# Queries turned on the host, keys and values as token rows, smaller score banks, a spread-out ranking and earlier first operands of the cosine layer

## The chip, the cores and the metric

The kernel runs on one core of one Trainium2 chip. The metric is the time of one execution on the device in microseconds (us), lower is better. The core has five engines that run their own instruction lists in order and wait for each other by semaphores: PE (matrix multiplies, from weights that are loaded into the array first; the loads are shown as PEld), DVE (vector), ACT (scalar), POOL and SP, which here mostly issues DMAs.

## The reference

```python
scores = (1 / sqrt(64)) * q @ k.T          # 8 batches, 8 heads, 576 tokens, head size 64
ret    = scores * gamma[h] ** (i - j)      # only for i >= j, else 0 (a decaying causal mask)
x      = (ret @ v)                         # -> 4608 tokens x 512
logits = x @ w_gate                        # 8 experts; each token goes to its best one
out[t] = gate[t] * (relu(x[t] @ w1[e]) @ w2[e])
h      = out @ w_in;  result = (h * cos(h)) @ w_out     # 512 -> 2048 -> 512, all tokens
```

All inputs are fp32 except the two matrices of the cosine layer, which arrive as 64-bit floats and are converted in the kernel.

## The kernel before

The program has three stages that follow one another.

**Attention and routing.** Each batch of 576 tokens is cut in five chunks, four of 128 tokens and one of 64, so there are 40 steps. Because the mask decays by a fixed factor, a chunk needs only itself (`intra`) and a carried 64x64 state per head (`inter`, from `sbd`). In iteration `i` the code issues `transposes(i+1)` (queries and decayed keys turned on PE into the PSUM tile `tp`, copied out by ACT), `scores(i)` (PE into `sc`, masked by DVE into `pT`), `decay_k(i+2)` (DVE), sometimes `unit_split` (an expert weight cut in two fp32r parts by ACT and DVE, 8 of the 40 iterations), `inter(i-1)` and `intra(i-1)` (PE into `xps`, scaled by DVE into `xt`), and `rows(i-2)` (PE turns the result back to token rows and makes the logits, into `rw`; ACT copies the rows out, then DVE sums the logits into `lgt`). `sc` and `rw` are the same PSUM buffer of two banks, with one copy, so the scores of an iteration wait until DVE has read the logits of the iteration before. Once a batch `route`, `place` and `spread`, in three iterations that follow each other, give every token a slot in its expert's list; they are small instructions on DVE and POOL. Loads of `q`, `k`, `v` are issued by SP four iterations ahead.

**Experts.** The experts are ranked by their count, and each takes a window of tokens in two halves (`hf`): `layer1` eight times, `layer2` four times, so 24 pieces, counted by `i`. At the first expert four bursts on DVE (`offsets`, `slots`, `excess`, and `turn_slots`, which has a PE transpose) finish the ranking behind the first four pieces; their scratch tile `room` takes one of the two `cvw` buffers. A background list (`bg`, some steps after each piece) converts the cosine layer's weights on DVE and ACT, with its loads (`conv_load`, into `cvw`) on SP. At the last expert SP loads the cosine layer's weights: `wide_unit` (8 pieces of 1 MB) and `ws_load(0)`, `ws_load(1)` (1.75 MB each, tile `wquad`, two buffers).

**Cosine layer.** A branch (`tc.If(late > 0)`, L1043, not taken here) stands ahead of it. Then 72 iterations (nine tiles of 512 tokens, eight column groups) run: seven products of 256 columns from `wquad` and operands that `enter` has put into a ring (`near`, `far`), with a cosine gate on ACT and DVE and the second matrix product `acc` (L1180). Four of the seven operands of a tile are differences (`turned`). The operands of the first tile are made behind the branch, the differences on POOL; those of later tiles at points of the loop named in `ahead`. `ws_load(i + 2)` is issued in iteration `i`.

Of the kernel before, what the change touches and what calls it, by code (L numbers as in the profile page):

```python
# [103 lines left out]

@with_exitstack
def attn_moe_kernel(ctx, tc, q, k, v, wg, w1, w2, win, wout, ctab, out):
    nc = tc.nc
    B = q.shape[0]
# [93 lines left out]
    with ExitStack() as actx:  # L202
# [3 lines left out]
        ps2 = actx.enter_context(tc.tile_pool(name="ps2", bufs=2, space=PSUM))  # L206
# [46 lines left out]
        for i in range(2):  # L253
            t = ap1.tile([P, NCH, E], F32, name=f"lgt{i}")
            nc.gpsimd.memset(t, 0.0)
            lgt.append(t)
# [5 lines left out]
        def load(i, nm):  # L262
            b, c = steps[i]
            o, n = CH[c]
            src = {"q": q, "k": k, "v": v}[nm]
            t = ap3.tile([P, H, D], F32, tag="ld" + nm, name="ld" + nm, bufs=6 if nm == "v" else 4)
            nc.sync.dma_start(out=t[:n], in_=src[b, :, o:o + n, :].rearrange("h t d -> t h d"))
            st[i][nm] = t

        def loads(i):  # L270
            for nm in "qkv":
                load(i, nm)
# [10 lines left out]
        def transposes(i):  # L283
            b, c = steps[i]
            o, n = CH[c]
            s = st[i]
            for nm in ("q", "kp"):
                pt = ps2.tile([P, 4, P], F32, tag="tp", name="tp")
                for j in range(4):
                    nc.tensor.transpose(pt[:, j, :n], s[nm][:n, 2 * j:2 * j + 2, :].rearrange("p a d -> p (a d)"),  # L290
                                        ident[:n, :n])
                t = ap3.tile([P, 4, P], F32, tag=nm + "T", name=nm + "T")
                nc.scalar.copy(out=t[:, :, :n], in_=pt[:, :, :n])
                s[nm + "T"] = t

        def scores(i):
# [4 lines left out]
            two = ps1.tile([P, 8, P], F32, tag="sc", name="sc")  # L301
            scs = [two[:, 0:4], two[:, 4:8]]
# [53 lines left out]
        def rows(i):  # L356
            b, c = steps[i]
            o, n = CH[c]
            two = ps1.tile([P, 8, P], F32, tag="sc", name="rw").rearrange("p (j a) t -> p j (a t)", a=2)
            for j in range(4):  # L360
                mm(out=two[:, j, 0:RW], lhsT=xts[i % 3][:, j, :], rhs=wgi[:, j, :], start=(j % 2 == 0), stop=True,
                   skip_group_check=True)
            x = ap3.tile([P, 4, P], F32, tag="xs", name="xs")
            if i < NS - 1:
                nc.scalar.copy(out=x[:n], in_=two[:n, :, 0:P])
            nc.vector.tensor_reduce(out=lgt[b % 2][:n, c, :], in_=two[:n, :, P:RW].rearrange("p j e -> p e j"),
                                    axis=AX.X, op=ALU.add)
            if i == NS - 1:
                nc.scalar.copy(out=x[:n], in_=two[:n, :, 0:P])
# [5 lines left out]
        def route(i0, n):  # L375

            b, c0 = steps[i0]
            L = lgt[b % 2][:, c0:c0 + n, :]
            sh = [P, n, E]
            mx = ap2.tile([P, n], F32, tag="mx", name="mx")  # L380
# [129 lines left out]
        load(0, "q")  # L510
        nc.sync.dma_start(out=ct, in_=ctab[:, :C_MASK])
        load(0, "k")
        nc.sync.dma_start(out=ca[:, :C_TRI - C_MASK], in_=ctab[:, C_MASK:C_TRI])
        load(1, "q")
        load(1, "k")
        load(0, "v")
        load(1, "v")
# [78 lines left out]
    def y_first():  # L596
        for g in range(2):
            nc.sync.dma_start(out=first[g], in_=ydT[2 * g * P:(2 * g + 2) * P, 0:512].rearrange("(a p) t -> p a t", p=P))

    with ExitStack() as mctx:  # L600
# [83 lines left out]
        cv = mctx.enter_context(tc.tile_pool(name="cv", bufs=1))  # L684
# [151 lines left out]
        def pick_slots(out, x):  # L836
            V.tensor_tensor(out=big, in0=hot.unsqueeze(2).to_broadcast([P, E, NBLK, E]),
                            in1=x.rearrange("p (e c) -> p c e", c=NBLK).unsqueeze(1).to_broadcast([P, E, NBLK, E]),
                            op=ALU.mult)
            V.tensor_reduce(out=out.rearrange("p (r c) -> p r c", c=NBLK), in_=big, axis=AX.X, op=ALU.add)  # L840

# [440 lines left out]
```

## Time and profile before

| | us |
|---|---|
| median of 3 runs (1454.59 to 1456.05) | 1454.84 |
| the profiled execution, its own time | 1457.35 |
| its span, first to last instruction | 1455.6 |
| PE busy | 1408.5 (97%) |
| PEld busy | 1306.1 (90%) |
| DVE busy | 959.1 (66%) |
| ACT busy | 714.3 (49%) |
| POOL busy | 229.2 (16%) |

The busy share is a mean over three stages with different limits, and a PE that the profile calls busy need not be at its peak. The profile's 40 slices show the granted PE clock at full speed except around 0 to 30, 200 to 270 and 673 to 691 us, that is at the start and at the two changes of stage. The span and the time of the profiled execution differ by 1.75 us, and that execution is 2.5 us above the median.

### The profile page before, as it was taken

The page shows a single profiled execution, that of the slowest core. Times are in us where ns is not written, and L with a number is a line of the kernel's source. Part 1 is how long each engine was busy: PE and PEld are TensorE (multiplying, and loading weights), DVE is VectorE, ACT ScalarE, POOL GpSimd, SP SyncE. Part 2 cuts the span into 40 slices and gives each one's busy share as a digit, 9 for nine tenths or more (in the row PEclk, how much of TensorE's full clock was granted, in tenths as well). Part 3 has the DMA queues.
Part 4 walks back from the last instruction along what each step waited for, and adds up shares of the span by engine and source line. Part 5 has one row for each costly group of instructions (what it writes and reads, how often), then busy time and mean ns, then how long its engine had stood idle before and what let it go on. Part 6 is the DMA issues. An engine that isn't in the chain of part 4 may idle for free.

```text
span 1455.6 us, 29059 instructions
## 1 busy us (share of the span) xinstructions
PE 1408.5 (97%) x11587; PEld 1306.1 (90%) x11587; DVE 959.1 (66%) x1900; ACT 714.3 (49%) x1405; POOL 229.2 (16%) x338
## 2 busy tenths in 40 slices
PE   8999987999999999997999999999999999999998
PEld 6888876999999999997899999999999999989896
DVE  4676765766777676843766667676766767666654
ACT  2344431445544545532655656555555556555544
POOL 3243341032221313201001010000101000010101
PEclk9999996999999999997999999999999999999999
DMA  9899853585777668776546464655656465555541
GB/s 190 205 220 225 216 128 97 166 263 176 250 221 225 218 188 265 255 256 254 203 163 249 158 254 153 226 187 185 227 178 235 167 231 173 205 202 193 191 165 67
DMA packets 179740, 292.25 MB, mean 201 GB/s; under 512 B 120612, under 2 KB 129264, under 8 KB 169360
## 3 DMA queue, kind: packets, MB, share of 16 engines
q1 hardware_dynamic: 166672, 248.33, 53.5%
q0 software_dynamic: 12928, 42.02, 8.4%
q8 instruction: 92, 1.51, 0.4%
q14 instruction: 48, 0.39, 0.1%
HBM read 238.85 MB, written 51.47 MB: 199 GB/s over the span
## 4 chain that ended last, share of the span: by engine, by line
PE 46%; issue 5%; DMA 1%; POOL 0%; DVE 0%; ACT 0%; POOLq 0%; ACTq 0%
PE acc L1180 24%; PE hps L1105 22%; DMA wquad<-ws 1%; POOL out_dram L1162 0%; DVE near L1090 0%; DVE far L1090 0%; POOLq L1278 0%; ACT ka L1135 0%; ACT near L1089 0%; POOL spare L143 0%; ACT orow L1160 0%; ACT gh L1146 0%; ACTq L1089 0%; POOLq L1162 0%
## 5 line engine op out<-in xcount | busy, mean ns | idle before, releaser
L1180 PE MATMUL acc<-wunit,gh 128*128 128x512 f32 x1152 | 358.4, 392 | 1.4 <-ACT gh L1146 1.4
L1180 PEld LDWEIGHTS acc<-wunit,gh 128*128 128x128 f32 x1152 | 207.3, 189 | 37.7 <-ACT gh L1146 1.8
L1105 PEld LDWEIGHTS hps<-far,wquad 128*128 128x128 f32 x1824 | 232.6, 192 | 6.2
L1105 PE MATMUL hps<-far,wquad 128*128 128x256 f32 x1824 | 237.3, 283 | 0.0
L1180 PE MATMUL acc<-wunit,gl 128*128 128x512 f32 x576 | 224.7, 390 | 0.0
L662 PE MATMUL hps<-xT,wunit 128*128 128x256 f32 (+6 forms) x1536 | 211.7, 299 | 0.7 <-ACT xT L647 0.7
L662 PEld LDWEIGHTS hps<-xT,wunit 128*128 128x128 f32 x1536 | 209.4, 191 | 1.3 <-ACT xT L647 1.1
L677 PE MATMUL hps<-hh,wunit 128*128 128x256 f32 (+6 forms) x1024 | 209.1, 299 | 0.2 <-ACT hh L665 0.2
L1105 PE MATMUL hps<-near,wquad 128*128 128x256 f32 x1200 | 161.8, 287 | 5.4 <-DVE near L1090 2.8
L1105 PEld LDWEIGHTS hps<-near,wquad 128*128 128x128 f32 x1200 | 156.7, 195 | 11.5 <-DVE near L1090 3.7
L677 PEld LDWEIGHTS hps<-hh,wunit 128*128 128x128 f32 x1024 | 165.3, 189 | 0.6 <-ACT hh L665 0.4
L677 PE MATMUL hps<-hl,wunit 128*128 128x256 f32 (+6 forms) x512 | 152.1, 297 | 0.8 <-DVE hl L666 0.7
L1162 POOL DMA_INDIRECT out_dram<-orow,perm x36 | 35.2, 977 | 727.9 <-DVE orow L1158 716.4
L1180 PEld LDWEIGHTS acc<-wunit,gl 128*128 128x128 f32 x576 | 108.2, 188 | 25.3 <-DVE gl L1148 1.6
L1142 DVE SCALAR_TENSOR_TENSOR sa<-sa,quad 128x512 f32<-128x512 f32 x144 | 99.1, 688 | 42.8 <-ACT sa L1140 42.8
L1146 ACT CAST gh<-sa 128x512 fp32r<-128x512 f32 x144 | 89.6, 622 | 72.5 <-DVE sa L1142 72.5
L1148 DVE TENSOR_TENSOR gl<-sa,gh 128x512 fp32r<-128x512 f32 x144 | 99.0, 688 | 23.0 <-ACT gh L1146 17.5
L1116 DVE TENSOR_TENSOR part<-hps,part 128x256 f32<-128x256 f32 x72 | 30.6, 425 | 120.1 <-PE hps L1105 120.0
L1137 DVE SCALAR_TENSOR_TENSOR sa<-quad,ka 128x512 f32<-128x512 f32 x144 | 99.0, 687 | 12.2 <-ACT ka L1135 12.2
L795 DVE TENSOR_TENSOR wunit<-wst,wunit 128x512 fp32r<-128x512 f32 x112 | 75.8, 687 | 36.2 <-ACT wunit L794 36.1
L677 PEld LDWEIGHTS hps<-hl,wunit 128*128 128x128 f32 x512 | 97.0, 189 | 1.4 <-DVE hl L666 1.4
L1139 ACT ACTIVATE sa<-sa 128x512 f32<-128x512 f32 x144 | 91.3, 634 | 9.0 <-DVE sa L1137 8.8
(196 smaller groups left out, 1900.0 us busy)
## 6 DMA issues: line engine op xcount, KB each, us to landing
wquad<-ws SPq DMA_DIRECT2D x72, 1792.0 KB
wst<-in_moe_w_dram SPq DMA_DIRECT2D x64, 512.0 KB
ws<-cvo POOLq DMA_DIRECT2D x56, 256.0 KB, 4.5
ldq<-in_q_dram SPq DMA_DIRECT2D x32, 256.0 KB
ldk<-in_k_dram SPq DMA_DIRECT2D x32, 256.0 KB
ldv<-in_v_dram SPq DMA_DIRECT2D x32, 256.0 KB
xd<-xs SPq DMA_DIRECT2D x32, 256.0 KB
cvw<-in_moe_w_in_dram SPq DMA_DIRECT2D x16, 512.0 KB
```

The costliest lines, as they stand in the source:

```text
L662: mm(out=ph[:, :n], lhsT=u[:, a, kc, f0:f0 + P], rhs=t[:, bq, kc, :n], start=(idx == 0), stop=(idx == 11))
L677: mm(out=py[:, :n], lhsT=u[:, w], rhs=t[:, :n], start=(fc == 0 and g == 0), stop=(fc == 7 and g == 2))
L795: nc.vector.tensor_sub(out=u[:, 1, 2 * g + c], in0=s[:, c], in1=u[:, 0, 2 * g + c])
L1105: mm(out=o, lhsT=u[:, s, kc, a], rhs=x[:, bq, kc], start=(s in (0, 1, 2) and idx == 0), stop=(idx == 5), skip_group_check=True)
L1116: nc.vector.tensor_add(out=u2, in0=y[:, :HT], in1=p1)
L1137: nc.vector.scalar_tensor_tensor(out=sa, in0=x, scalar=INV2PI, in1=ka, op0=ALU.mult, op1=ALU.subtract)
L1139: nc.scalar.activation(out=sa, in_=sa, func=AF.Sin, scale=math.pi)
L1142: nc.vector.scalar_tensor_tensor(out=sa, in0=sa, scalar=-1.0, in1=x, op0=ALU.add, op1=ALU.mult)
L1146: nc.scalar.copy(out=gh, in_=sa)
L1148: nc.vector.tensor_sub(out=gl, in0=sa, in1=gh)
L1162: ins = nc.gpsimd.indirect_dma_start(out=out[:, :], out_offset=bass.IndirectOffsetOnAxis(ap=perm[:, k:k + 1], axis=0), in_=o, in_offset=None)
L1180: mm(out=acc2[T][c], lhsT=pair[n][:, fh, c % 2 * P:(c % 2 + 1) * P], rhs=u[:, w, fc % 4], start=(q == 0 and fh == 0 and n == 0 and w == 0) ...
```

## The change

1. The host hands over the queries already turned (`qt`: 128 partitions, 2 KB each of a chunk in one piece) and keys and values as token rows (`kv`: 4 KB in one piece per token). One load brings both `k` and `v`. The PE transposes of the queries and their ACT copies go. The order of the first loads is different.
2. The two-bank buffer of scores and rows is replaced by three single banks in rotation: the two halves of the scores take one each, and so do the two halves of the rows. `rows` now has two ACT copies and two logit sums of half the width, and `route` adds the two sums. The single bank for transposes pays for the third.
3. `offsets`, `slots` and `excess` become one background job `prepare`, taken in small steps ahead of the conversions. `turn_slots` moves from piece 3 to piece 14 of the first expert.
4. `first_operands` makes the differences and the first four operands of the first cosine tile in the second half of the last expert, on ACT and DVE, in tiles that the conversions leave free. Three operands are still made behind the branch. The ring has 12 places and no longer 13. `wide_unit` loads are issued at pieces 0, 2, ... 14 (before: 0, 3, ... 21), and `ws_load(1)` moves behind the branch.

```diff
-        def load(i, nm):
-            src = {"q": q, "k": k, "v": v}[nm]
-            t = ap3.tile([P, H, D], F32, tag="ld" + nm, name="ld" + nm, bufs=6 if nm == "v" else 4)
-            nc.sync.dma_start(out=t[:n], in_=src[b, :, o:o + n, :].rearrange("h t d -> t h d"))
+        def load_q(i):
+            t = ap3.tile([P, 4, P], F32, tag="ldq", name="ldq", bufs=6)
+            nc.sync.dma_start(out=t[:, :, :n], in_=qt[b, :, 4 * o:4 * (o + n)].rearrange("p (j t) -> p j t", j=4))
+        def load_kv(i):
+            t = ap3.tile([P, 2, H, D], F32, tag="ldkv", name="ldkv", bufs=6)
+            nc.sync.dma_start(out=t[:n].rearrange("p s h d -> p s (h d)"), in_=kv[b * SEQ + o:b * SEQ + o + n])
...
-            for nm in ("q", "kp"):
-                pt = ps2.tile([P, 4, P], F32, tag="tp", name="tp")
+            pt = ps1.tile([P, 4, P], F32, tag="tp", name="tp")
...
-            two = ps1.tile([P, 8, P], F32, tag="sc", name="sc")
-            scs = [two[:, 0:4], two[:, 4:8]]
+            scs = [ps1.tile([P, 4, P], F32, tag="sc", name="sc", bufs=3) for g in range(2)]
...
+            for g in range(2):
+                two = ps1.tile([P, 4, P], F32, tag="sc", name="rw", bufs=3).rearrange("p (j a) t -> p j (a t)", a=2)
+                for j in range(2):
+                    mm(out=two[:, j, 0:RW], lhsT=xts[i % 3][:, 2 * g + j, :], rhs=wgi[:, 2 * g + j, :], start=(j == 0),
+                       stop=True, skip_group_check=True)
+                nc.scalar.copy(out=x[:n, 2 * g:2 * g + 2], in_=two[:n, :, 0:P])
+                nc.vector.tensor_reduce(out=lgt[b % 2][:n, c, g, :], in_=two[:n, :, P:RW].rearrange("p j e -> p e j"),
+                                        axis=AX.X, op=ALU.add)
...
+    def first_operands():
+        turned(0, 1)
+        yield
+        turned(0, 2)
+        enter(0, 0)
+        yield
+        turned(0, 3)
+        enter(0, 1)
+        yield
+        turned(0, 4)
+        enter(0, 2)
+        yield
+        enter(0, 3)
+        yield
...
-        bg += [conv(n) for n in range(NCV)]
+        bg += [prepare()] + [conv(n) for n in range(NCV)]
...
-                elif i % 3 == 0:
-                    wide_unit((0, 2, 1, 3)[i // 6], i // 3 % 2, nc.sync)
+                elif i % 2 == 0 and i < 16:
+                    wide_unit((0, 2, 1, 3)[i // 4], i // 2 % 2, nc.sync)
...
-                if e + 1 == E and i in (16, 20):
-                    ws_load(i // 20)
+                if e + 1 == E and i == 16:
+                    ws_load(0)
...
-                if e == 0 and i < 4:
-                    (offsets, slots, excess, turn_slots)[i]()
+                if e == 0 and i == 14:
+                    turn_slots()
...
-    for n in (2, 3, 5):
+    ws_load(1)
+    for n in (4, 5, 6):
         enter(0, n)
```

On PE, one whole attention step of a later chunk read before as follows (`tp` are the transposes, first of the queries, then of the keys; `xps` is the carried and the own part, `S` the new state, `rw` the rows of two steps earlier):

```order
L290 MATMUL tp<-ct,ldq 128x128 x4
L290 MATMUL tp<-ct,kp 128x128 x4
L307 MATMUL sc<-qT,kpT 64x128 x16
L332 MATMUL xps<-qT,sbd_131 64x128 x8
L342 MATMUL xps<-pT,ldv 64x128 x8
L351 MATMUL S<-ldv,kp 64x64 x8
L361 MATMUL rw<-wgi,xt_125 128x136 x4
```

and reads now:

```order
L307 MATMUL tp<-ct,kp 128x128 x4
L323 MATMUL sc<-ldq,kpT 64x128 x16
L348 MATMUL xps<-ldq,sbd_129 64x128 x8
L358 MATMUL xps<-pT,ldkv 64x128 x8
L367 MATMUL S<-ldkv,kp 64x64 x8
L379 MATMUL rw<-wgi,xt_126 128x136 x4
```

The four query transposes are gone, the rest stands in its place, and `sc` and `xps` read the loaded queries themselves.

On ACT, around the end of the last expert and the branch (L1043), the list before was (`hh` and `yev` leave the expert's two layers):

```order
L665 ACTIVATE hh<-hps 128x232 x8
L679 COPY yev<-hps 128x232
...
L679 COPY yev<-hps 128x232 x3
L1043 COMPARE_AND_BRANCH
...
L1089 CAST near<-yfirst 128x512 x3
L1089 CAST far<-turn 128x512
L1089 CAST near<-turn 128x512 x2
L1089 CAST far<-turn 128x512
```

and is now (the branch is L1112):

```order
L725 ACTIVATE hh<-hps 128x232 x3
L642 CAST near<-yfirst 128x512
L725 ACTIVATE hh<-hps 128x232
L642 CAST near<-yfirst 128x512
L725 ACTIVATE hh<-hps 128x232
L642 CAST near<-turn 128x512
L725 ACTIVATE hh<-hps 128x232
L642 CAST near<-turn 128x512
...
L1112 COMPARE_AND_BRANCH
...
L642 CAST far<-yfirst 128x512
L642 CAST far<-turn 128x512 x2
```

Four of the seven casts have moved in between those of the last expert's first layer; three are left behind the branch.

On SP, the same place before (`wunit` from `wd` are the `wide_unit` loads, `wquad` the `ws_load`s, `ydT` the expert's results, `sidT` a small list of tokens, `yraw` the next tile's input):

```order
L803 DMA wunit<-wd_71 128x2048 x2
L808 DMA wquad<-ws_74 128x3584
L803 DMA wunit<-wd_73 128x2048
...
L808 DMA wquad<-ws_74 128x3584
...
L803 DMA wunit<-wd_73 128x2048
...
L1043 COMPARE_AND_BRANCH
...
L1186 DMA sidT<-idc 36x128
L1072 DMA yraw<-ydT 128x2x512 x2
L808 DMA wquad<-ws_74 128x3584 x2
```

and now:

```order
L862 DMA wunit<-wd_73 128x2048 x2
L867 DMA wquad<-ws_74 128x3584
...
L741 DMA ydT<-yev 128x232
L1112 COMPARE_AND_BRANCH
...
L1224 DMA sidT<-idc 36x128
L867 DMA wquad<-ws_74 128x3584
L624 DMA yraw<-ydT 128x2x512 x2
L867 DMA wquad<-ws_74 128x3584 x2
```

All `wunit` loads now stand ahead of the first `wquad`, and the second `wquad` stands behind the branch.

## Rows read from the trace of the kernel before

**Rows 1.** Windows by stage: us, busy time by engine, granted clock, DMA share, GB/s.

```profile
30.00:200.00 170.00, 162.75 (x2992) 145.79 (x2993) 115.76 (x291) 70.14 (x150) 57.74 (x84) 1.00 0.91 213
235.00:270.00 35.00, 30.75 (x211) 29.34 (x211) 26.27 (x72) 10.47 (x24) 3.65 (x4) 0.86 0.50 151
701.00:1456.00 755.00, 746.31 (x4656) 674.05 (x4656) 494.49 (x884) 421.20 (x781) 38.35 (x72) 1.00 0.52 190
```

**Rows 2.** Waits from 30 to 200 us: who for whom, us, times, longest.

```profile
DVE lgt L366 <- ACT xs L365: 27.4, 27, 1.4
...
PEld sc L307 <- DVE lgt L366: 8.7, 27, 0.7
...
DVE kp L280 <- DMA ldk<-in_k_dram: 0.5, 1, 0.5
```

**Rows 3.** Timeline of an attention step: start, us, engine, instruction, [idle before it].

```profile
100.38 1.21 DVE L190 TENSOR_TENSOR wunit<-wst,wunit 128x1024 fp32r<-128x1024 f32 x1
...
102.50 0.86 PEld L307 LDWEIGHTS sc<-qT,kpT 64*64 64x64 f32 x32 [0.29 <-DVE lgt L366]
...
103.77 1.27 DVE L311 TENSOR_TENSOR pT<-sc,ca 128x512 f32<-128x512 f32 x2
...
105.46 0.99 PEld L361 LDWEIGHTS rw<-wgi,xt 128*128 128x128 f32 x8
...
105.57 0.68 DVE L345 TENSOR_TENSOR xt<-xps,gx 128x512 f32<-128x512 f32 x1
105.63 0.37 ACT L354 COPY sbd<-S 128x256 f32<-128x256 f32 x1 [2.74 <-PE S L351]
106.38 0.47 PEld L290 LDWEIGHTS tp<-ct,ldq 128*128 128x128 f32 x4
...
106.69 0.59 ACT L365 COPY xs<-rw 128x512 f32<-128x512 f32 x1 [0.69 <-PE rw L361]
...
107.31 0.19 DVE L366 TENSOR_REDUCE lgt<-rw 128x8 f32<-128x32 f32 x1 [1.07 <-ACT xs L365]
...
107.55 0.54 PEld L307 LDWEIGHTS sc<-qT,kpT 64*64 64x64 f32 x15 [0.27 <-DVE lgt L366]
```

**Rows 4.** Timeline of the start, third keys and second scores.

```profile
15.39 0.69 DVE L280 TENSOR_TENSOR kp<-ldk,ca 128x512 f32<-128x512 f32 x1 [2.91 <-DMA ldk<-in_k_dram]
...
17.25 1.99 PE L307 MATMUL sc<-qT,kpT 64*64 64x128 f32 x32
```

**Rows 5.** Windows around the stage changes, columns as in the first group.

```profile
245.00:265.00 20.00, 17.80 (x118) 16.80 (x118) 14.66 (x35) 6.83 (x15) 3.10 (x3) 0.83 0.57 179
660.00:670.00 10.00, 10.00 (x92) 10.00 (x91) 1.14 (x3) 2.92 (x6) 0.00 (x0) 1.00 0.94 363
675.00:690.00 15.00, 9.24 (x37) 7.50 (x37) 8.96 (x9) 4.67 (x9) 6.22 (x4) 0.50 0.37 114
```

**Rows 6.** Waits of PE from 235 to 265 us.

```profile
PE tp L878 <- DVE sidf L840: 2.1, 1, 2.1
PE tp L644 <- DVE xT L648: 1.2, 1, 1.2
```

**Rows 7.** Waits of SP from 235 to 250 us.

```profile
SPq L694 <- DVE hl L666: 9.2, 1, 9.2
```

**Rows 8.** Timeline of ACT and PE from the last expert to the cosine layer.

```profile
675.08 0.35 ACT L679 COPY yev<-hps 128x232 f32<-128x232 f32 x1 [4.43 <-DMA ydT<-yev]
675.53 1.87 PE L199 MATMUL hps<-ct 128*128 128x256 bf16 x8 [2.63 <-ACTq L1043]
...
679.11 1.66 ACT L1089 CAST near<-yfirst 128x512 fp32r<-128x512 f32 x3 [3.67 <-SPq L1043]
...
679.78 0.80 PE L1105 MATMUL hps<-near,wquad 128*128 128x256 f32 x2 [2.38 <-ACT near L1089]
...
692.50 3.76 PE L1105 MATMUL hps<-near,wquad 128*128 128x256 f32 x30
```

**Rows 9.** Chain that ended last, around 693 us: start, us, what.

```profile
692.70 8.16 DMA wquad<-ws
```

More of the change, by code (lines that the diff above doesn't have):

```diff
@@ L253, in attn_moe_kernel @@
         for i in range(2):
-            t = ap1.tile([P, NCH, E], F32, name=f"lgt{i}")
+            t = ap1.tile([P, NCH, 2, E], F32, name=f"lgt{i}")
             nc.gpsimd.memset(t, 0.0)
@@ L286, in transposes @@
             s = st[i]
-            for nm in ("q", "kp"):
-                pt = ps2.tile([P, 4, P], F32, tag="tp", name="tp")
[L289 to L294, printed above, removed]
+            pt = ps1.tile([P, 4, P], F32, tag="tp", name="tp")
+            for j in range(4):
+                nc.tensor.transpose(pt[:, j, :n], s["kp"][:n, 2 * j:2 * j + 2, :].rearrange("p a d -> p (a d)"),
+                                    ident[:n, :n])
+            t = ap3.tile([P, 4, P], F32, tag="kpT", name="kpT")
+            nc.scalar.copy(out=t[:, :, :n], in_=pt[:, :, :n])
+            s["kpT"] = t
         def scores(i):
@@ L377, in route @@
             b, c0 = steps[i0]
-            L = lgt[b % 2][:, c0:c0 + n, :]
             sh = [P, n, E]
+            L = ap2.tile(sh, F32, tag="L", name="L")
+            nc.vector.tensor_add(out=L, in0=lgt[b % 2][:, c0:c0 + n, 0, :], in1=lgt[b % 2][:, c0:c0 + n, 1, :])
             mx = ap2.tile([P, n], F32, tag="mx", name="mx")
@@ L508, in attn_moe_kernel @@
         tabled = []
-        load(0, "q")
+        load_kv(0)
+        nc.sync.dma_start(out=ca[:, :C_TRI - C_MASK], in_=ctab[:, C_MASK:C_TRI])
         nc.sync.dma_start(out=ct, in_=ctab[:, :C_MASK])
[L512 to L517, printed above, removed]
+        load_q(0)
+        loads(1)
         nc.sync.dma_start(out=gx[:, 0].rearrange("p j t -> p (j t)"), in_=ctab[:, C_GX:])
@@ L874, in excess @@
             V.tensor_copy(out=toti, in_=totf)
+            yield
         def turn_slots():
@@ L1046, in attn_moe_kernel @@
         y_first()
+        for _ in first_operands():
+            pass
     warm(NWARM3, psA.tile([P, 512], F32, tag="h", name="hps", bufs=4), ident)
-    yp = ctx.enter_context(tc.tile_pool(name="yp", bufs=1))
     rowp = ctx.enter_context(tc.tile_pool(name="rowp2", bufs=3))
     gp = ctx.enter_context(tc.tile_pool(name="gp", bufs=3))
-    HT = 256
-    NQ = 8
     NALL = NTILE * NQ
-    NSLOT = 7
-    ring = []
-    near = yp.tile([P, 5, 2, 2, HT], F32R, name="near")
-    ring += [near[:, n] for n in range(5)]
     for m in range(2):
```

119 lines of the change are left out of this document (64 added, 55 removed).

## The prediction

> **What bounds the kernel now.** I read the windows by stage first [rows 1]. In the cosine stage PE is busy for 746 of 755 us at the full clock, and the change leaves its products alone, so nothing is to be won there. That leaves the attention stage, the two changes of stage, and the start. In attention PE is busy for 163 of 170 us, DVE for 116, and the DMA engines for 91% of the time at 213 GB/s. A reader may take the loads for the limit, so I looked at the waits next [rows 2]: one instruction waited once for a load, 0.5 us in 170. The loads were just hidden. What PE waits for is the PSUM buffer of scores and rows: 8.7 us in 27 waits, and behind that DVE's sums wait 27.4 us for ACT's copy of the same buffer. So the step is PE's own list plus that wait.
>
> The timeline of one step shows its parts [rows 3]. Scores start at 102.50 and the next ones at 107.55, a period of 5.05 us. The query transposes take 0.44 of it (106.38 to the key transposes, which the row's 0.47 overlaps a little), and the wait for the sums 0.27.
>
> At the two changes of stage the clock is the second loss: 0.83 of full speed from 245 to 265 us, and 0.50, which is the 1.2 GHz level, from 675 to 690 [rows 5].
>
> **Attention, step by step.** PE's part of a full step becomes 5.05 - 0.44 - 0.27 = 4.34 us, if nothing else takes the wait's place. The new banks make a new chain, and I place it from the start of the scores, T. The rows' eight passes start at T + 2.96 and issue in 0.99; ACT's copy starts 0.24 behind their issue [rows 3]. With half the rows in a bank, four passes and 0.24 put the first copy at T + 3.70. A copy of 256 columns takes 0.37 (the `sbd` row), the sum 0.19, and some 0.08 of hand-over: the second bank of the next scores is free at T + 4.34. So chain and PE tie, and the wait can go as a whole. The second half's copy and sum end later, but the next user of that bank is far off. DVE alone is through with `xt` at T + 3.75, 0.32 before the first copy ends.
>
> Per batch of four full steps and a half one, the transposes give 4 x 0.44 + 0.22 = 2.0 us and the waits 8.7 / 34 x 5 = 1.3 (34 steps lie in the window), together 3.3. I take off 0.3, since the step behind the half chunk is short on PE and the chain then sets it. The three routing iterations of a batch put small DVE work between the last sum and the next mask; DVE has 0.32 us of room. This costs between nothing and the whole 0.7 of a step; I take 0.2 for each, nearer to the room. That leaves 2.4 a batch, and 37 steps (all but the first three) make 7.4 batches: 17.8 us. In the eight iterations that split a weight DVE has 1.21 us more ahead of `xt` [rows 3]; there the chain through DVE is the limit already and no part of it is shortened, so these eight win nothing: 8 x 0.6 = 4.8 less. **Attention: -13 us**, with -2 (every routing step loses its 0.7) and -22 (neither cost shows) as bounds. The extra instructions on ACT (a second copy) take less than the query copies that go.
>
> **Start.** The third keys reach DVE at 15.39 after a wait of 2.91 for their load, and the second scores start at 17.25 [rows 4]. Counted from the code, 2.8 MB are issued up to that load before and now. At 213 GB/s they need 13.3 us, at the 363 GB/s of a stretch with large pieces [rows 1, 5] 7.8. Bounds 0 and -5.5; I take **-3**, about the middle, since the constants between are in smaller pieces as before.
>
> **Last rows of attention.** The last step used to sum before it copied; now both copies come first (0.37 of the second is exposed), and the two sums are added. **+0.5 us**.
>
> **First expert.** PE waited 2.1 us for the transpose of the slots and 1.2 for a late `xT` on the crowded DVE [rows 6]. Meanwhile SP stood 9.2 us in front of a conversion load [rows 7], whose buffer the ranking's scratch held, and the next expert's weights queued behind it and then came in one bunch. Spread out, the transpose is met ten pieces later, and the conversion load is issued only when the scratch is free, so neither wait has a cause left. The clock fell behind these waits: 20 us at 0.83 lose 3.4 us [rows 5]. Together 6.7; I take **-6**, bounds -2.1 (the transpose alone) and -6.7. The ten steps of ranking are added to the background list, which still ends before piece 12 of the last expert; the DVE work is the same, and from then on it lies beside PE's products.
>
> **Into the cosine stage.** PE ends the last expert at 672.9 (2.63 before its next instruction). ACT's last copy waited 4.43 for a store behind big loads and ended at 675.43, the first operand started at 679.11, 3.7 later, because its tile waits for SP to pass the branch, and the second iteration of the loop started at 692.50 [rows 8]. Now four operands are ready, the big loads are out earlier, so the copy ends near 673.4, and products can run through while DVE and ACT make the other three. But `ws_load(1)` has moved behind the branch: SP passes it 3.7 after the copy, at 677.1, and such a load took 8.16 from issue to use [rows 9]. The second iteration then starts at 685.3, not at 692.5: -7.2. PE stands for some 3 us before it and starts at the low clock, which I price at 1.2. **-6 us**, bounds 0 (load in traffic, a wait as long as the old one) and -9 (SP through the branch sooner). The work of the early operands lies in the last expert's second half, where DVE is busy 1.14 of 10 us [rows 5].
>
> **Sum**: -3 - 13 + 0.5 - 6 - 6 = -27.5 us. From the profiled execution's own 1457.35 us this is 1429.9; that execution is 2.5 above the median of the runs, so the time is **1427 us**.
>
> **The rivals.** (A) The forecast, 0.55. (B) DVE sets the attention step: its small routing work and the later second sum make every routing step lose its gain. For it speaks that DVE is busy 68% now and its work stays while the time shrinks; against it that it still waits for ACT 27 us. Attention then gives 3 and the time is 1437: 0.17. (C) The second `wquad` comes late, or ACT's copies queue as before, and the cosine stage starts no earlier: 1433, 0.14. B and C together: 1443, 0.03. (D) Slower: the clock. If the DVE-bound steps leave PE standing, it may fall to 1.2 GHz in the attention stage. Two stalls in the first expert, the two waits of PE there, lost 3.4 us of clock, 1.7 each [rows 5, 6]; 32 steps can be late (24 routing, 8 splitting), which costs up to 54, and 16 such falls eat the whole gain. At 54 the time is 1481. Against it: waits of about 0.3 us in a step now leave the stage at clock 1.00 [rows 1, 3]. 0.04. The Trainium skill's "TensorE: Matmul & The Clock Gate", section "A second HAM failure mode: psum-queue depth-cycling", tells of a kernel that cycled through PSUM banks and whose clock fell and rose again and again; it speaks against the rotating banks, and only the run can say whether this stage is dense enough. (E) The loads were the limit after all: 170 us at 213 GB/s become 100 at 363, 70 instead of 13, and the time is 1370: 0.02; the 0.5 us of load waits speak against it [rows 2]. The Trainium skill's "DMA: Bandwidth & Descriptors", section "Specifications", asks for transfers of at least 512 B for the full rate, where one head's row is 256 B, and gives 358 GB/s as the HBM limit of a core; by that page alone the stage would win 69 us. The trace does not bear it out as a limit, since hardly anything waits for these loads. (F) Everything in attention that I took as a cost hides, and the start takes its upper bound: 1415, 0.03. (G) Nothing moves, because a wait equal to each removed one appears: 1455, 0.02.
>
> **Chances and range.** Faster by over 0.2%, which is about what a measurement of this kernel can tell from no change: A, B, C, both, E and F, 0.94. Within 0.2%: G, 0.02. Slower: D, 0.04. The bounds of all terms at once give 1412 to 1451. The range of 1414 to 1441 takes in A with its terms off by half, B, C and F, and leaves out D, E, G and most of B with C.
>
> **What would show it.** Right: the attention stage at about 4.7 us a step (30 to 200 us held 34 steps before), PE's wait for `lgt` near nothing outside the splitting iterations, clock 1.00; the first `sc` rows some 3 us earlier; no `sidf` wait in the first expert, and SP not standing in front of `cvw`; four `near` casts ahead of the branch, and the second iteration of products waiting for `wquad`. Wrong: `lgt` or `pT` waits in every step (B), a granted clock under 1.00 between 30 and 180 us (D), an iteration in the cosine stage that is longer than before, since the ring is one place shorter and its reuse comes one product sooner, or PE waiting for `ldkv` or `ldq`.

## The result and the profile after

The changed kernel takes 1419.68 us (median of 4 runs, 1419.5 to 1421.04) and the kernel before 1455.44 beside it (4 runs): a ratio of 0.9755, 95% interval 0.9738 to 0.9772, some 36 us faster. The forecast was 1427.

The windows of the changed kernel, in the columns of [rows 1]:

```profile
30.00:170.00 140.00, 134.54 (x2609) 120.23 (x2601) 109.55 (x302) 56.85 (x136) 59.12 (x84) 1.00 0.74 236
214.00:224.00 10.00, 9.48 (x78) 9.27 (x79) 7.98 (x30) 4.22 (x11) 1.20 (x2) 1.00 0.48 154
224.00:234.00 10.00, 10.00 (x89) 10.00 (x88) 9.44 (x25) 4.94 (x11) 2.87 (x3) 1.00 0.52 145
235.00:270.00 35.00, 35.00 (x226) 34.91 (x225) 23.93 (x45) 13.85 (x28) 2.94 (x4) 1.00 0.52 167
637.00:660.00 23.00, 17.59 (x132) 16.99 (x132) 5.34 (x11) 6.50 (x15) 0.00 (x0) 0.85 0.63 238
660.00:1418.00 758.00, 751.18 (x4691) 678.66 (x4689) 499.26 (x892) 424.46 (x787) 38.11 (x72) 1.00 0.52 190
```

In attention the clock stays at 1.00, DVE's share has risen from 68% to 78%, and the DMA engines need 0.74 of the time for 236 GB/s where they needed 0.91 for 213. The first expert, whose products start at 214.3 here (234.7 before), has hardly any idle PE and no low clock left. The low clock at the second change of stage is still there (0.85).

The waits of the changed kernel in attention, columns as in [rows 2]:

```profile
DVE lgt L382 <- ACT xs L381: 9.5, 36, 0.4
...
PEld sc L323 <- issue: 4.2, 25, 0.2
...
PEld sc L323 <- DVE lgt L382: 4.0, 5, 1.0
```

PE's wait for the sums has become rare: 5 times in 140 us, each time in the step behind the split of a weight. What is left in most steps is a gap of 0.17 us between the weight loads (PEld) for which the profile names nobody. It is not new: the seven steps of the kernel before that had no wait for the sums show the same gap, in the view of [rows 2]:

```profile
PEld sc L307 <- issue: 1.2, 7, 0.2
```

One step, as in [rows 3]:

```profile
135.21 1.10 PE L323 MATMUL sc<-ldq,kpT 64*64 64x128 f32 x32
...
138.94 0.84 ACT L381 COPY xs<-rw 128x256 f32<-128x256 f32 x2 [0.22 <-DMA ldkv<-in_kv_dram]
...
139.34 0.17 DVE L382 TENSOR_REDUCE lgt<-rw 128x8 f32<-128x16 f32 x1 [0.20 <-ACT xs L381]
139.73 0.62 PE L323 MATMUL sc<-ldq,kpT 64*64 64x64 f32 x13
```

The period is 4.52 us. The first copy starts 3.73 behind the scores and the first sum ends 4.30 behind them, which the forecast had put at 3.70 and 4.26.

The change of stage to the cosine layer, as in [rows 8, 9] (the last two lines are of the chain that ended last):

```profile
643.64 0.35 ACT L739 COPY yev<-hps 128x232 f32<-128x232 f32 x1 [2.05 <-PE hps L737]
...
645.51 3.12 PE L1143 MATMUL hps<-near,wquad 128*128 128x256 f32 x24
...
646.38 0.62 ACT L642 CAST far<-yfirst 128x512 fp32r<-128x512 f32 x1 [2.39 <-SPq L1112]
...
655.19 5.21 PE L1143 MATMUL hps<-near,wquad 128*128 128x256 f32 x24 [4.42 <-DMA wquad<-ws]
...
647.22 7.83 DMA wquad<-ws
655.06 0.14 issue
```

The copy no longer waits for a store, and the products start some 2 us behind its start. The second iteration stands 4.42 us for the load that left behind the branch, and its first 24 products then take 5.21 us, where an undisturbed iteration needs 3.04.

To see where the time went I took the same instructions in each trace as marks: the third scores, the last scores, the first expert's first product, the last expert's last product, the start of the loop's third iteration, and PE's last instruction. The differences between marks, in us, worked out from the timelines of each run (the experiments follow below):

```
                 third   to last  to first  to last   to third   to PE's
                 scores  scores   expert    expert    iteration  end
before            21.89   185.69   27.08    437.97     28.37     747.33
after             17.10   168.50   28.70    428.99     22.26     745.30
e1_two_bank       21.09   182.05   27.76    429.86     22.12     745.81
e2_turned_twice   19.81   178.02   28.69    427.99     23.53     745.33
e3_small_loads    19.60   168.09   27.49    431.35     22.96     745.00
e4_burst          19.77   168.32   27.82    436.67     21.95     745.34
e5_operands_late  18.53   168.19   28.59    428.52     20.97     745.22
e6_wquad20        18.95   168.11   26.94    431.63     18.98     744.90
e7_wquad23        18.03   169.44   28.46    431.54     23.77     744.92
e8_split_late     17.41   175.30   29.98    429.74     22.99     745.05
e9_split_pool     20.56   169.74   28.62    428.02     22.98     745.04
e10_wquad20_y3    20.35   168.27   26.66    429.44     20.47     745.33
e11_split_gaps    19.25   165.07   28.43    428.57     21.25     745.16
e12_both          19.30   165.06   28.69    429.34     20.64     746.30
```

From before to after the columns give -4.8, -17.2, +1.6, -9.0, -6.1 and -2.0, together -37.5 of the 37.9 us by which the two spans differ. One trace of each kernel stands behind a row, and the first column shows how much such a number strays: nine of the experiments (e4 to e12) start with the changed kernel's instructions up to this mark, and with it they lie between 17.1 and 20.6. That stray goes with the granted clock from 5 to 20 us: it was 1.00 in the changed kernel and e8 (mark at 17.1 and 17.4), 0.89 in e5 to e7 (18.0 to 19.0), 0.77 in e4, e11 and e12 (19.3 to 19.8) and 0.66 in e9 and e10 (20.6 and 20.4). In the kernel before it was 0.89.

### The profile page after: what moved, and what is told of

The parts are those of the page before. It is cut to its first block, busy times and chain, and to the rows that moved or that the text cites. A ratio compares the mean times of both kernels' runs of the same rounds, so it can differ in the third digit from the quotient of the medians.

```text
span 1417.7 us, 28604 instructions
## 1 busy us (share of the span) xinstructions
PE 1381.1 (97%) x11427; PEld 1284.0 (91%) x11427; DVE 964.5 (68%) x1953; ACT 705.6 (50%) x1405; POOL 223.0 (16%) x334
## 4 chain that ended last, share of the span: by engine, by line
PE 42%; issue 11%; POOL 1%; DMA 1%; ACT 0%; POOLq 0%
PE acc L1218 22%; PE hps L1143 20%; POOL out_dram L1200 1%; DMA wquad<-ws 1%; PE hps L212 0%; POOLq L1310 0%; POOL spare L156 0%; ACT ka L1173 0%; ACT orow L1198 0%; ACT gh L1184 0%; PE acc L1229 0%; POOLq L1200 0%
## 5 line engine op out<-in xcount | busy, mean ns | idle before, releaser
L1143 PEld LDWEIGHTS hps<-far,wquad 128*128 128x128 f32 x1920 | 244.6, 191 | 7.3
L1143 PE MATMUL hps<-far,wquad 128*128 128x256 f32 x1920 | 249.3, 283 | 0.0
L722 PE MATMUL hps<-xT,wunit 128*128 128x256 f32 (+6 forms) x1536 | 208.6, 296 | 0.9 <-ACT xT L707 0.7
L722 PEld LDWEIGHTS hps<-xT,wunit 128*128 128x128 f32 x1536 | 206.4, 188 | 1.4 <-ACT xT L707 0.9
L1143 PE MATMUL hps<-near,wquad 128*128 128x256 f32 x1104 | 147.5, 286 | 4.4 <-DMA wquad<-ws 4.4
L1143 PEld LDWEIGHTS hps<-near,wquad 128*128 128x128 f32 x1104 | 142.9, 194 | 8.2 <-issue 4.6
L1186 DVE TENSOR_TENSOR gl<-sa,gh 128x512 fp32r<-128x512 f32 x144 | 98.9, 687 | 20.4 <-ACT gh L1184 14.9
L1153 ACT COPY part<-hps 128x256 f32<-128x256 f32 x72 | 26.8, 372 | 144.2 <-PE hps L1143 137.9
```

Of the source, the lines that this page charges most:

```text
L722: mm(out=ph[:, :n], lhsT=u[:, a, kc, f0:f0 + P], rhs=t[:, bq, kc, :n], start=(idx == 0), stop=(idx == 11))
L1143: mm(out=o, lhsT=u[:, s, kc, a], rhs=x[:, bq, kc], start=(s in (0, 1, 2) and idx == 0), stop=(idx == 5), skip_group_check=True)
L1153: nc.scalar.copy(out=p1, in_=x[:, :HT])
L1186: nc.vector.tensor_sub(out=gl, in0=sa, in1=gh)
```

## The experiments

All of them are the changed kernel with one edit. Each time is the median of its runs, with the ratio to the kernel before on the same chip.

**e1_two_bank.** One buffer of two banks again, with one copy and one sum:

```diff
-            scs = [ps1.tile([P, 4, P], F32, tag="sc", name="sc", bufs=3) for g in range(2)]
+            two = ps1.tile([P, 8, P], F32, tag="sc", name="sc")
+            scs = [two[:, 0:4], two[:, 4:8]]
...
```

> The changed kernel with one part undone: scores and rows share one two-bank buffer again, with one copy and one sum; everything else as changed. Theory (chain): in a full step the scores wait for the chain rows, one copy of 512 columns (0.59 us), sum; this chain does not hold the query transposes, so without the three banks their removal wins next to nothing, the step stays near 5.0 us and attention loses about 16 of its 17 us: 1436 us, and PE's waits for the sums are longer than before the change (near 0.7 us a step instead of 0.27). Rival (the two parts add up): only the waits come back, 1.3 us a batch: 1429 us, waits of 0.27 a step.

Measured: 1435.41 us, ratio 0.9860 (0.9844 to 0.9877). Waits of this kernel from 30 to 170 us, and one step:

```profile
DVE lgt L382 <- ACT xs L381: 23.5, 23, 1.4
...
PEld sc L324 <- DVE lgt L382: 17.0, 27, 1.1
```

```profile
148.60 1.10 PE L324 MATMUL sc<-ldq,kpT 64*64 64x128 f32 x32 [0.40 <-DVE lgt L382]
...
152.79 0.59 ACT L381 COPY xs<-rw 128x512 f32<-128x512 f32 x1 [0.69 <-PE rw L379]
153.41 0.19 DVE L382 TENSOR_REDUCE lgt<-rw 128x8 f32<-128x32 f32 x1 [1.07 <-ACT xs L381]
153.65 0.48 PEld L324 LDWEIGHTS sc<-ldq,kpT 64*64 64x64 f32 x13 [0.70 <-DVE lgt L382]
```

The period is 5.05 us, exactly that of [rows 3], although four transposes are gone: the wait has grown by the time that they took. The chain theory stands, the sum of the parts falls. Attention gains 3.6 of 17.2 us without the new banks, nearly all of it in the seven steps, one a batch, in which PE had not waited for the sums before (an ordinary one took 5.08 us and takes 4.64).

**e2_turned_twice.** The key transposes are done twice:

```diff
-            for j in range(4):
+            for j in (0, 1, 2, 3, 0, 1, 2, 3):
                 nc.tensor.transpose(pt[:, j, :n], s["kp"]...
```

> The changed kernel with the key transposes of each chunk done twice, so that PE has four more passes a step, as many as the query transposes that went. Theory (PE's own list is the limit of the attention step now): 0.44 us a full step and 0.22 a half one, 2.0 a batch, over 37 steps 14.8: 1434 us. Rival (the chain through ACT's copy and DVE's sum is the limit, PE has room): under 5 us more, at most 1425.

Measured: 1431.49 us, ratio 0.9837 (0.9821 to 0.9854). The five steps of a batch take, where no split lengthens them, 4.33, 4.52, 4.88, 4.96 and 5.08 us in this trace, together 23.77, and 3.89, 4.09, 4.62, 4.52 and 4.65 in the changed kernel's, together 21.77: 2.0 a batch, as PE's own list asks. In the steps lengthened by a split the extra passes cost nothing (5.03 us in the fifth of the eight, 5.02 in the changed kernel), so attention loses 9.5 and not 14.8 us. PE is the limit of an ordinary step, and the chain through DVE that of a splitting one.

**e3_small_loads.** Keys and values by heads, in pieces of 256 B (the queries stay in large pieces):

```diff
...
-            nc.sync.dma_start(out=t[:n].rearrange("p s h d -> p s (h d)"), in_=kv[b * SEQ + o:b * SEQ + o + n])
+            for s in range(2):
+                nc.sync.dma_start(out=t[:n, s], in_=kv[s, b, :, o:o + n, :].rearrange("h t d -> t h d"))
```

> The changed kernel with keys and values handed over by heads, so that their loads come in pieces of 256 B again, in two DMAs a chunk; queries stay turned. Theory (the loads are just hidden at the old speed, and the shorter stage needs more): the stage moves 236 GB/s now, the old pieces gave 213 at 0.91 of the DMA engines' time, so loads are waited for in the attention stage: the start loses 3 to 5 us and attention 3 to 15, 1426 to 1439. Rival (loads stay hidden): the start alone, third scores at 20 to 22 us instead of 17.1, 1423 to 1425.

Measured: 1421.68 us, ratio 0.9769 (0.9752 to 0.9785), not to be told from the changed kernel. Its window in attention:

```profile
30.00:170.00 140.00, 134.88 (x2595) 120.65 (x2592) 110.29 (x305) 57.26 (x137) 57.57 (x83) 1.00 0.90 237
```

The theory fell. The same 237 GB/s go through with keys and values in 256-B pieces; the DMA engines are busy for 0.90 of the time instead of 0.74, attention takes 168.1 us as before the edit, and the third scores at 19.60 lie within the stray of the others. 213 GB/s was what the old, slower stage asked for and not what such pieces allow.

**e4_burst.** The ranking in bursts behind the first three pieces, `turn_slots` at the fourth:

```diff
...
+                if e == 0 and i < 3:
+                    for _ in range((2, 4, 9)[i]):
+                        next(ready, 0)
-                if e == 0 and i == 14:
+                if e == 0 and i == 3:
                     turn_slots()
```

> The changed kernel with the ranking in bursts behind the first three pieces of the first expert again, and the transpose of the slots at piece 3. Theory (the prediction's step): the transpose is waited for 2.1 us, an operand 1.2, SP stands some 9 us before a conversion load, and the clock falls behind these waits, 3.4: plus 6 to 7, 1426 us. Rival (the first expert won by the clock at its start, which was 0.69 before and 1.00 after, not by the ranking): the waits alone come back, plus 2 to 3, 1422, and the clock stays at 1.00 from 225 to 245 us.

Measured: 1428.39 us, ratio 0.9811 (0.9794 to 0.9828). Waits of PE in the first 430 us of its experts, and its windows:

```profile
PE tp L941 <- DVE sidf L900: 2.1, 1, 2.1
PE tp L704 <- DVE xT L708: 1.5, 2, 1.2
```

```profile
215.00:225.00 10.00, 6.96 (x55) 6.34 (x54) 8.85 (x32) 2.75 (x7) 1.57 (x2) 1.00 0.16 48
225.00:235.00 10.00, 10.00 (x73) 9.83 (x71) 5.04 (x17) 3.08 (x7) 1.51 (x2) 0.83 0.51 163
235.00:245.00 10.00, 7.89 (x48) 7.25 (x48) 9.76 (x21) 3.74 (x9) 1.75 (x2) 0.83 0.61 195
```

The wait of 2.1 and the low clock behind it are back, as the prediction had them: 20 us at 0.83 are 3.4 us. SP's stand in front of the conversion load is back too, in its waits from 205 to 270 us:

```profile
SPq L753 <- DVE hl L726: 8.3, 1, 8.3
```

In all, the experts take 7.7 us longer than in the changed kernel. The rival falls, though what it names exists: here the stage starts at the full clock.

**e5_operands_late.** None of the first operands is made in the last expert:

```diff
-                    bgs.append(first_operands())
...
     ws_load(1)
+    for _ in first_operands():
+        pass
     for n in (4, 5, 6):
         enter(0, n)
```

> The changed kernel with all seven first operands made behind the branch (the differences on DVE), none in the last expert. Theory (the second weight load sets the start of the cosine stage): the second iteration waits for the load that SP issues behind the branch until 655.2 us with or without early operands, so at most 2 us are lost: 1420 to 1422. Rival (the early operands are the gain): products start 4 to 5 us later as in the kernel before and stay late: 1425.

Measured: 1419.12 us, ratio 0.9751 (0.9734 to 0.9767). PE of this kernel:

```profile
647.69 0.51 PE L1140 MATMUL hps<-near,wquad 128*128 128x256 f32 x2 [1.63 <-ACT near L642]
649.10 5.07 PE L1140 MATMUL hps<-near,wquad 128*128 128x256 f32 x22 [0.90 <-DVE near L643]
653.96 2.77 PE L1140 MATMUL hps<-far,wquad 128*128 128x256 f32 x18
656.56 0.64 PE L1140 MATMUL hps<-near,wquad 128*128 128x256 f32 x4
```

The products start later and run into the second iteration without a stop, about when the load (issued at 647.93) lands anyway. Part 4's early operands win nothing here.

**e6_wquad20** and **e7_wquad23.** The second load ahead of the branch, at piece 20 or behind the last store (the edit of e6; e7 has 23 for 20):

```diff
-                if e + 1 == E and i == 16:
-                    ws_load(0)
+                if e + 1 == E and i in (16, 20):
+                    ws_load(int(i > 16))
...
-    ws_load(1)
```

> The changed kernel with the second load of cosine weights back at piece 20 of the last expert, ahead of the branch. Theory: the wait of 4.4 us for this load and the low clock behind it (24 products in 5.2 instead of 3.0 us) go: minus 6, 1414 us. Rival (the wait moves): the expert's last stores queue behind the load, ACT waits for them as in the kernel before (4.4 us), the branch comes later by as much, and nothing is won: 1419 to 1421.

> The changed kernel with the second load of cosine weights behind the last store of the last expert and ahead of the branch. Theory: the load leaves when the last store has left, some 3 us sooner than behind the branch, and no store stands behind it: the wait of 4.4 shrinks to 1 to 2, and with it the low clock: minus 3 to 5, 1415 to 1417. Rival (the load is late because of traffic, not of its issue): 1419 to 1421.

Measured: e6 1418.93 us, ratio 0.9752 (0.9736 to 0.9768), e7 1425.07, ratio 0.9794 (0.9777 to 0.9810). ACT of e6, then of e7:

```profile
648.42 0.35 ACT L739 COPY yev<-hps 128x232 f32<-128x232 f32 x1 [4.63 <-DMA ydT<-yev]
```

```profile
657.20 0.62 ACT L642 CAST far<-yfirst 128x512 fp32r<-128x512 f32 x1 [9.03 <-SPq L1112]
```

In e6 the rival is right in kind: the last copy waits 4.63 us for a store behind the load. The change of stage still shrinks by 3.3 us, but the experts take 2.6 longer in this trace: between 560 and 580 us the clock is at 0.91 behind a wait of 1.2 for an operand, where the changed kernel waited 0.9 and kept 1.00. In e7 both theories fell: SP passes the branch only some 9 us after it has issued the load, about as long as such a load takes to land (7.83), and the three late operands wait 9.03 us for that. It makes the change of stage 1.5 us longer. Another 2.5 of e7's loss lie in the experts; there the same instructions as in the changed kernel started at a low clock:

```profile
216.00:226.00 10.00, 10.00 (x59) 0.68 0.48 154
```

**e8_split_late.** The split of a weight behind the rows of its iteration:

```diff
-            if i >= 9 and (i - 9) % 4 == 0 and (i - 9) // 4 < len(wq):
-                unit_split(*wq[(i - 9) // 4], upA)
...
                 rows(i - 2)
+            if i >= 9 and (i - 9) % 4 == 0 and (i - 9) // 4 < len(wq):
+                unit_split(*wq[(i - 9) // 4], upA)
```

> The changed kernel with the split of an expert weight (ACT's copy, DVE's difference of 1.21 us) moved behind the rows of its iteration, so that it stands behind the two sums and no longer ahead of the scaling of the outputs. Theory (in the eight splitting iterations DVE's 1.21 us lie in the chain to the sums and to the next scores): each of them loses its extra 1.1 us: minus 6 to 9, 1411 to 1414, and the waits of scores for sums, 4.0 us between 30 and 170 us, go. Rival (DVE is the limit there in any order): the mask of the next scores comes later by as much and nothing is won: 1418 to 1421.

Measured: 1429.29 us, ratio 0.9818 (0.9801 to 0.9835): worse by some 10 us. Windows around two of its bad places (columns as above), and DVE and PE at the first:

```profile
70.00:75.00 5.00, 4.29 (x77) 3.58 (x75) 3.80 (x12) 2.55 (x5) 3.11 (x6) 1.00 0.72 242
75.00:80.00 5.00, 3.98 (x69) 3.52 (x68) 1.72 (x5) 1.12 (x3) 2.39 (x5) 0.67 0.62 197
```

```profile
71.41 1.22 DVE L203 TENSOR_TENSOR wunit<-wst,wunit 128x1024 fp32r<-128x1024 f32 x1 [0.77 <-ACT wunit L202]
...
73.90 0.74 DVE L327 TENSOR_TENSOR pT<-sc,ca 64x256 f32<-64x256 f32 x2
...
74.36 0.73 PE L379 MATMUL rw<-wgi,xt 128*128 128x136 f32 x4 [0.71 <-DVE pT L327]
```

Here the split falls between the sums and the small ranking work of a batch, the next mask comes late, PE stands 0.71 and then 1.02 us, and the clock falls to 0.67: two steps of 6.98 and 5.16 us where 4.64 and 3.89 are usual. Both theories fall: order matters, but this order is worse. Where the split met no ranking work it was hidden in its own step (steps 9 and 29: 4.68 and 4.69), and the step behind took 4.46 and 4.15 where 3.89 is usual.

**e9_split_pool.** The difference on POOL, in its old place:

```diff
-    def unit_split(key, g, pool):
+    def unit_split(key, g, pool, eng):
...
-        nc.vector.tensor_sub(out=u[:, 1, 2 * g:2 * g + 2], in0=s, in1=u[:, 0, 2 * g:2 * g + 2])
+        eng.tensor_sub(out=u[:, 1, 2 * g:2 * g + 2], in0=s, in1=u[:, 0, 2 * g:2 * g + 2])
...
-                unit_split(*wq[(i - 9) // 4], upA)
+                unit_split(*wq[(i - 9) // 4], upA, nc.gpsimd)
```

> The changed kernel with the difference of an expert weight's split (1.21 us on DVE, eight times in the attention stage) made by POOL, at the same place of the code. Theory (in the splitting iterations DVE's own list is the limit, and the place in it only decides who is late): seven of the eight steps are 0.7 to 1.2 us longer than the same step of another batch, 7.0 us in all, and these go: 1412 to 1414. Rival (POOL and DVE get in each other's way, or POOL's placing work comes late behind the difference): nothing won or worse, 1419 to 1430.

Measured: 1421.86 us, ratio 0.9770 (0.9754 to 0.9786), nothing won. The trace of POOL and DVE:

```profile
73.47 2.36 POOL L203 TENSOR_TENSOR wunit<-wst,wunit 128x1024 fp32r<-128x1024 f32 x1
...
74.19 1.66 DVE L479 TENSOR_SCALAR gts<-gts 128x5 f32<-128x5 f32 x1
```

Five elements a partition, which take 0.26 us at the median of their line in this kernel, took 1.66: the instruction ended at 75.85, when POOL's ended at 75.83. The rival is right, and the last section says how.

**e10_wquad20_y3.** e6, with a free tile of the conversions as a third buffer for the results:

```diff
+            if (e, hf, dc) == (E - 1, 1, 2):
+                y = cv.tile([P, 512], F32, tag="cvx", name="yev")
...
```

> The kernel of e6_wquad20 with a third buffer for the results of the last half expert (a free tile of the conversions), so that ACT's last copy waits for a store that was issued ahead of the big load. Theory (e6 gained its 4.4 us of load wait and gave most of it back, because the last copy waited 4.63 us for a store behind the load): the products start some 2 us after PE's last expert product, as in the changed kernel, and the second iteration needs no load: minus 4 to 5 from the changed kernel, 1415. Rival (the branch holds back what stands behind it until load and stores have landed): the three operands made behind the branch come late instead, PE waits for them, and nothing is won over e6: 1418 to 1420.

Measured: 1417.46 us, ratio 0.9743 (0.9726 to 0.9759). The copy's wait is gone, but the products start no sooner than in e6. The chain that ended last shows why not:

```profile
645.58 0.60 PE hps L212 x4
646.18 2.92 issue
649.10 1.03 PE hps L212 x4
```

PE stops in the middle of its warm-up passes behind the branch, for 2.92 us in which the profile shows no one to wait for. The result lies between theory and rival. The interval overlaps the changed kernel's.

**e11_split_gaps** and **e12_both.** Splits behind the rows, in iterations of short chunks and two behind such, which have no ranking work at that place; and the same together with e10:

```diff
+        split_at = [9, 14, 19, 20, 24, 29, 34, 35]
...
                 rows(i - 2)
+            if i in split_at:
+                unit_split(*wq[split_at.index(i)], upA)
...
```

> The changed kernel with the weight splits behind the rows, as in e8_split_late, but only in the iterations of short chunks (9, 14, 19, 24, 29, 34) and in two that follow one (20, 35), where DVE has no ranking work of a batch between the sums and the next mask. Theory (e8 lost where the split met that routing work, and hid the split where it did not: its steps 9 and 29 were 4.68 and 4.69 us against 4.64, the steps behind them 0.3 and 0.6 longer): the splits cost about 4 us in place of 7, no step is over 5.3 us, clock 1.00: 1416 to 1418. Rival (moving the split moves the same delay into the step behind it): 1420 or more.

> e10_wquad20_y3 and e11_split_gaps together. Theory (two places of the program that do not meet): the two gains add up, 2 us of e10 and 3 of e11: 1414 to 1416, faster than both kernels. Rival (what is won ahead of a stage change is given back there): 1417 to 1420.

Measured: e11 1416.79 us, ratio 0.9739 (0.9724 to 0.9753), e12 1414.51, ratio 0.9712 (0.9698 to 0.9726). In both traces attention takes 165.1 us, 3.4 less than in the changed kernel, as e11's theory had it. e11's interval still overlaps the changed kernel's. e12 is faster than both kernels: its interval and the changed kernel's (0.9738 to 0.9772) do not touch. PE stops for 2.84 us behind the branch there too.

## Why the prediction was right, and where it was not

The forecast's case A came true, and its range held. The sum was 10 us short against the traces (-27.5 forecast, -37.9 in the spans; against the medians the time is 7 us under the 1427), in the following steps.

**Attention, -13 forecast, -17.2 measured.** The tie of PE and chain at 4.34 us was right in kind: the chain came out within 0.05 us, and PE's list is 0.17 longer because of the small gaps "issue" ahead of the scores, which the old wait had covered. By batch, three terms were mis-sized. The waits gave about 0.6 us and not 1.3: of the 8.7 us of [rows 2], 0.17 in each of the 27 waits is this gap, which stays. The routing term, 0.2 for each of three iterations, does not show: the steps of a batch take 3.89, 4.09, 4.62, 4.52 and 4.65 us where [rows 3]'s kernel had 4.71, 4.66, 5.10, 5.05 and 5.08, and the three that hold routing work (the second to the fourth) win 0.57, 0.48 and 0.53, the transposes (0.44, 0.22 and 0.44) and some wait. And the step behind the half chunk, the first, for which 0.3 was taken off, wins the most: a wait that stood there before, 0.2 us in an ordinary batch, has gone (in the view of [rows 2]).

```profile
PE rw L361 <- DVE pT L311: 2.3, 7, 1.0
```

So a batch wins 2.8 and not 2.4, and 7.4 batches 20.9. The splits took 3.7 of that back, where the forecast had 4.8: over 7.4 batches of such steps the stage was longer by 3.7 us before (185.69 - 7.4 x 24.6) and is by 7.4 now (168.50 - 7.4 x 21.77). e11 brings this back to 4.0. e8 shows that rival D's price was real: the clock does fall in this stage once DVE's work is put into the wrong gap. The changed kernel keeps clear of it.

The forecast wrote the gain as 2.0 for transposes and 1.3 for waits. e1 and e2 show that they are no two gains: transposes alone win 3.6 us, the banks alone (with the same PE work put back) 7.7, both 17.2.

**Start, -3 forecast, -4.8 in this trace.** Over the changed kernel and the experiments that share its first 20 us (e4 to e12) the mark is at 18.9 on average, which is -3.0; over e5 to e7, which had the clock of the kernel before (0.89), it is at 18.5, which is -3.4. The rest of the -4.8 is a better clock in that one trace, and luck. The reason was wrong, or not shown: the forecast had it from the larger pieces, and e3, with keys and values in small ones, starts no later (19.60) than the kernels with its clock of 0.77 (19.3 to 19.8). The missing transposes may be a part of it: e2, with as many passes put back, has the mark at 19.81 at a clock of 0.89, where e5 to e7 have 18.0 to 19.0. The order of the loads and the pieces of the queries were not tried alone.

**Last rows, +0.5 forecast, +1.6 in this trace.** The same instructions took 26.7 to 28.7 us in the six traces that leave the splits alone (after, e4 to e7, e10), 27.9 on average or +0.8.

**First expert, -6 forecast, -9.0 measured.** e4 gives 7.7 of it back, by the mechanism named: the wait for the transpose, and the clock behind it. What the forecast left out is the clock at the start of the stage, 0.68 from 234.66 to 240.00 in the kernel before, 1.00 here: 1.7 us. It is no merit of the change, since e7 had it low with the same instructions.

**Into the cosine stage, -6 forecast, -6.1 measured.** The second iteration waits for the load behind the branch as forecast: SP issues it 3.2 us behind the end of the last copy (forecast 3.7) and it takes 7.83 (8.16). The 24 products at the low clock cost 2.2 where the forecast had 1.2. But one reason was wrong: the forecast gave the four ready operands a part in it, and e5 does without them at no loss. What won is that the last copy has no store to wait for ([rows 8] had 4.43), since the large loads leave earlier, and, as far as the traces tell, that the differences are made on DVE instead of POOL. No run parts the two, but the trace of e5 gives their sizes: from the last expert's last product to the first product of the loop it takes 3.9 us where the kernel before took 7.2, and the first iteration takes 8.9 instead of 12.7. In that iteration of the kernel before, DVE's instructions for the operands took 1.3 to 1.8 us each while POOL made the differences, and 0.68 when POOL was through:

```profile
679.76 4.63 DVE L1090 TENSOR_TENSOR near<-yfirst,near 128x512 fp32r<-128x512 f32 x3 [16.74 <-ACT near L1089]
...
683.80 1.71 POOL L1083 TENSOR_TENSOR turn<-yfirst,turn 128x512 f32<-128x512 f32 x1
...
687.19 0.68 DVE L1090 TENSOR_TENSOR far<-turn,far 128x512 fp32r<-128x512 f32 x1
```

It looks like what e9 shows in the attention stage, where DVE waits for POOL (last section).

**Cosine loop, nothing forecast, -2.0 measured.** In the trace before two of the iterations are 1.0 and 1.5 us longer than the rest, and PE waits there for a gate (0.45 and 0.96 us); the thirteen traces of the changed code need 744.9 to 746.3 us from the third iteration on. One point of the order for the next tile's operands has moved there. Whether that is the cause was not tried and stays open; these 2 us, too, are luck to the forecast.

**The rivals.** B (DVE sets the routing steps) and E (loads were the limit) are out by the steps above and by e3, C by the 22.26 us of the change of stage (28.37 before). On E the Trainium skill's "DMA: Bandwidth & Descriptors", section "Specifications", asks for 512 B and more at the full rate. The run agrees that small pieces cost DMA time (0.90 busy for 237 GB/s against 0.74 for 236) and shows that nothing waited for it. The Trainium skill's "TensorE: Matmul & The Clock Gate", section "A second HAM failure mode: psum-queue depth-cycling", tells of a kernel that cycled through PSUM banks and whose clock fell and rose. That did not happen here: with three banks in rotation the granted clock was 1.00 from 30 to 170 us. F, with 1415, was the nearest of the rivals, because most of the costs that the forecast had put into attention did hide.

## What to carry to other kernels

Two things that lengthen one step are not two gains: write the step as the larger of PE's list and of each chain, since what is taken off one of them is worth little until the other is shorter too. Work that is moved to an idle gap has to be checked against what else uses that gap in other iterations; the same 1.2 us of DVE work cost 0.9 us (7.4 by eight), 0.5 (4.0 by eight in e11), or 3.6 with the clock (steps 14 and 15 of e8), by its place alone. Ahead of a branch, a load in flight was not free here: in e6 it held a store, in e7 what stands behind the branch came late, and in e10 and e12 PE stopped, for a reason that is open.

## What the runs showed of the hardware

**DVE waits for POOL, and not always.** In e9 each of the eight differences on POOL (2.36 us) held one DVE instruction until POOL was done: a product of two SBUF operands of usually 0.68 us took 1.34 to 2.31 in six cases, a scalar product of five elements 1.66 in two. Masks that read PSUM (0.68 to 0.69 each) and reductions ran beside POOL at their usual time. This is how the Trainium skill's "SBUF — State Buffer", section "SBUF: two separate sides", has it: the port pair that the two engines share is locked for a whole instruction, and only some forms of DVE instruction need it. The run agrees. Rivals of that kind belong into a forecast that moves work to POOL.

**The clock behind equal waits is not equal.** An operand of the seventh expert was waited for 1.2 us in e3, e6 and e10; the clock from 560 to 580 us was 0.91, 0.91 and 1.00. Such differences of 2 us lie in the rows of the table above, and single traces should not be compared more closely.

**PE stops behind a branch under a load.** In e10 and e12, where the second load was issued 7.7 us before PE passed the branch, PE stopped for 2.92 and 2.84 us among eight equal passes; in the changed kernel, in which no such load was out, for 0.40. In e6 the load was issued 10 us before, and PE did not stop. The profile shows no releaser. What PE waits for there is open. One candidate is the code behind the branch: the traces list a few DMA packets of a kind called `instruction` around it, and in e7, where SP came late, none ran from 649.5 to 653.7 us, under the big load, and two from 653.7 to 655.1, some 2 us ahead of what stands behind the branch. No run tried it.
